# Moving one tile's q and k loads from SyncE's DMA queue into GpSimd's, in a fused retention and Mish MLP kernel on one Trainium2 core

## The chip, the cores and the metric

The kernel runs on one core of a Trainium2 chip. A core has TensorE (matrix products and transposes), VectorE, ScalarE (casts and activations), GpSimd (elementwise work on SBUF) and SyncE (here only an issuer of DMAs). DMAs are issued by an instruction in the queue of SyncE, ScalarE or GpSimd; 16 DMA engines move the data of all of them. In this kernel a DMA that casts float32 to bfloat16 on the way is always issued by GpSimd.

The metric is the device time of one execution in microseconds (us). Each engine runs its own instructions in the order in which they are issued; waits between engines are semaphores. In the profile PE is TensorE, PEld its weight loads, DVE is VectorE, ACT is ScalarE, POOL is GpSimd, SP is SyncE. `q0` in the DMA view is the queue that GpSimd feeds, `q1` the one that SyncE feeds.

## What is computed

```python
# q, k, v: (8 batches, 8 heads, 576 positions, 64), float32
scores = (1 / sqrt(64)) * q @ k.T
gamma  = 1 - 2.0 ** (-5 - arange(8))                 # one per head
Dmat   = where(i >= j, gamma ** (i - j), 0)
attn   = (scores * Dmat) @ v                         # retention, no softmax
x      = attn.transpose(0, 2, 1, 3).reshape(4608, 512)
h      = x @ w_in                                    # w_in (512, 2048)
out    = (h * tanh(softplus(h))) @ w_out             # Mish; w_out (2048, 512), out float32
```

## The kernel before

The 576 positions of a batch are cut into chunks of 128 (the last one has 64, and two batches share one). 36 chunks in all make nine tiles of four chunks, that is 512 rows of `x` each. Tiles 0 and 1 are the first chunks of the eight batches. They need no state from earlier positions, only scores times the decay mask times v. All others are computed with a running state: `state` (L359) multiplies k and v of a chunk (L373), and `step_o` adds q times the state.

For every tile follow two products. `g1(t, f)` (L407) computes 128 of the 2048 hidden columns in four matmuls of 512 rows (L412) and lets ScalarE apply Mish (L414); 16 calls make a tile. `g2` multiplies by `w_out`, for tile 0 in `g2_first` (L438, matmuls L444): here `part` 0 to 3 needs one quarter of `w_out` each, for all four chunks of the tile.

**Tile 0.** SyncE and ScalarE load q and k of tile 0 in pieces of one head (L124 to L127), GpSimd loads five of k's heads with a cast (`load_first_k`, L103, the tile `kb`), then SyncE loads v (L128, `load_first_v(0)`). Casts, transposes (`f_transpose`), scores and masks (`f_scores`) follow. `f_v(0, b, engine)` (L260) casts v of batch b to bfloat16, for b 0 to 2 on GpSimd and for b 3 on ScalarE; `f_out(0, b)` (L265) multiplies and copies the result to `xT`, the left side of `g1`.

**Weights.** GpSimd loads `w_in` with a cast in five DMAs: columns 0 to 255, 256 to 511, and three times 512 (L497 to L504, issued by L86). The casts of v stand between the first ones in GpSimd's queue. `w_out` follows in four DMAs of four row blocks each (L508, issued by L89).

**Tile 1.** `load_second_qk` (L107) issues 16 DMAs of 128 KB on SyncE, in two groups g of four heads: four of q and four of k for each group, all float32. They land in `stage`, a tile with the name `gT`, which held tile 0's q and k and then its masked scores; so they wait for `f_out(0, ...)`. `s_cast(g)` (L226) casts a group on VectorE, `s_transpose(g)` (L234, matmuls L239) transposes it, `s_scores` (L246) multiplies and masks. Tile 1's v comes in four DMAs of 256 KB by GpSimd (`load_first_v(1)`, L511), and `f_v(1, b)` casts it on ScalarE.

**Order on TensorE.** After tile 0's 16 `g1` calls comes the loop at L523, with tile 0's 16 `g2_first` calls and between them the steps for tile 1: `T0` (transposes of group 0) ahead of call 0, `S0 C1` (scores of group 0, cast of group 1) ahead of call 3, `T1` ahead of 9, `S1` ahead of 11, v's casts ahead of 12, the four `f_out(1, ...)` ahead of 14 and 15. Then follow tile 1's `g1` calls, with the first chunks of the later tiles between them.

**GpSimd's queue.** After the `w_in` and `w_out` issues it holds `make_masks` (four small operations), `load_first_v(1)`, `load_k0(0)` (k of batch 0 with positions in the partitions, for the first state), and for b 0 to 3 `f_state(0, b)` (L281, v scaled for the state, L285) and `load(8 + b)` (three DMAs: q, k, v of one later chunk, L303). `step_v` (L316) and more loads follow, one chunk at a time.

Of the kernel before, what the change touches and what calls it, by code (L numbers as in the profile page):

```python
# [10 lines left out]
F32 = mybir.dt.float32  # L11
# [6 lines left out]
def kernel(  # L18
# [18 lines left out]
    nc = tc.nc  # L37
    B, H, S, D = q.shape
    assert (B, H, S, D) == (8, 8, 576, 64)
    P = 128  # L40
# [3 lines left out]
    nF = d_ff // P  # L44
# [40 lines left out]
    def load_w_in(f0, n):  # L85
        nc.gpsimd.dma_start(out=w_in_t[:, :, ds(f0, n)], in_=w_in_r[:, :, ds(f0, n)])  # L86

    def load_w_out(i):
        nc.gpsimd.dma_start(out=w_out_t[:, ts(i, 4), :], in_=w_out_r[:, ts(i, 4), :])  # L89
# [4 lines left out]
    stage = gp.tile([P, nF, NCH * P], BF16, name="gT")  # L94
    raw = {0: (stage[:, 0:H, :].bitcast(F32), stage[:, H:nF, :].bitcast(F32))}
# [8 lines left out]
        for h in hs:  # L104
            nc.gpsimd.dma_start(out=kb0[:, h, :], in_=rows(k, 0, h))

    def load_second_qk():  # L107
        raw[1] = (stage[:, H:nF, :].bitcast(F32), stage[:, 0:H, :].bitcast(F32))
        for g in range(2):
            for i, x in enumerate((q, k)):  # L110
                for p in (2 * g, 2 * g + 1):
                    for e in range(2):
                        to = raw[1][i][:, ds(2 * p, 2), :].rearrange("(j e) a c -> j e (a c)", e=2)
                        nc.sync.dma_start(
                            out=to[:, e],
                            in_=x[4:8, 2 * p + e, 0:P, :].rearrange("b (g r) d -> g b (r d)", r=8))

    def load_first_v(t):
        for b in range(4 * t, 4 * t + 4):
            v0[b] = io.tile([P, H, D], F32, name="vraw", bufs=8)  # L120
            (nc.gpsimd if t else nc.sync).dma_start(out=v0[b], in_=v[b, :, 0:P, :].rearrange("h p d -> p h d"))
# [46 lines left out]
    def make_masks():  # L168
        nc.gpsimd.memset(mask, 1.0)
        nc.gpsimd.affine_select(out=mask, in_=mask, compare_op=OP.is_ge, fill=0.0,  # L170
                                base=0, pattern=[[1, P]], channel_multiplier=-1)
        nc.gpsimd.tensor_copy(mask2, mask)
        nc.gpsimd.memset(mask2[0:64, 64:P], 0.0)

    def keep_warm(n, pool=ps_o, name="ops"):
        idle = pool.tile([P, 512], F32, name=name)
        for _ in range(n):
            nc.tensor.matmul(idle, lhsT=zeros[:, 0:P], rhs=zeros, start=True, stop=True)
# [81 lines left out]
    def f_v(t, b, copy):  # L260
        vb = first.tile([P, H, D], BF16, name="vb", bufs=4)
        copy(vb, v0[4 * t + b])
        fst[t]["vb"][b] = vb

    def f_out(t, b, copy):  # L265
        if b == 0:
            xts[t] = xp.tile([P, KC, NCH * P], BF16, name="xT")
        vb = fst[t]["vb"][b]
        if t == 0 and b < 2:
            pool, name = ((ps_st, "st"), (ps_o, "ops"))[b % 2]  # L270
            ot = pool.tile([P, NP, P], F32, name=name)
        else:
            ot = ps_sc.tile([P, 2, NP, P], F32, name="sc")[:, 0]
        for p in range(NP):
            for e in range(2):
                nc.tensor.matmul(ot[ds(64 * e, 64), p, :], lhsT=vb[:, 2 * p + e, :],
                                 rhs=fst[t]["sm", 2 * p + e][:, b, :],
                                 start=(p == 0), stop=True, skip_group_check=True)
        copy(xts[t][:, :, ts(b, P)], ot)

    def f_state(t, b, engine=nc.gpsimd):  # L281

        n = 4 * t + b
        v0s[n] = first.tile([P, H, D], BF16, name="v0s", bufs=B)
        engine.tensor_tensor(v0s[n], v0[n], gv[:, 0, :].unsqueeze(2).to_broadcast([P, H, D]), op=OP.mult)  # L285

    def load_k0(b):
        k0[b] = first.tile([P, H, D], BF16, name="k0", bufs=B)
        nc.gpsimd.dma_start(out=k0[b], in_=k[b, :, 0:P, :].rearrange("h p d -> p h d"))  # L289
# [3 lines left out]
    def load(n):  # L293
        if n >= n_chunks:
            return
        b, c = chunks[n]
        qr = io.tile([P, H, D], F32, name="qraw")
        vr = io.tile([P, H, D], F32, name="vraw", bufs=8)
        qks = io.tile([P, 2, H, D], BF16, name="qks", bufs=9)
        live[n] = {"q": qr, "v": vr, "qks": qks}  # L300
        for t, src in ((qr, q), (qks[:, 1], k), (vr, v)):
            if c < 4:
                nc.gpsimd.dma_start(  # L303
                    out=t, in_=src[b, :, ds(P * c, P), :].rearrange("h p d -> p h d"))
            else:
                for e in range(2):
                    nc.gpsimd.dma_start(  # L307
                        out=t[ds(64 * e, 64)],
                        in_=src[b + e, :, ds(512, 64), :].rearrange("h p d -> p h d"))
# [167 lines left out]
    dve, act, pool = nc.vector.tensor_copy, nc.scalar.copy, nc.gpsimd.tensor_copy  # L477
# [16 lines left out]
            f_cast(n, act)  # L494
    keep_warm(3, ps_h, "hp")
    nc.scalar.activation(warm, pos[:, 0:1], AX.Mish)
    load_w_in(0, 256)  # L497
    f_v(0, 0, pool)
    f_v(0, 1, pool)
    load_w_in(256, 256)  # L500
    f_v(0, 2, pool)
# [2 lines left out]
        load_w_in(512 * i, 512)  # L504
    for b in range(4):
        f_out(0, b, (dve, act)[b % 2])
    load_second_qk()
    for i in range(4):  # L508
        load_w_out(i)
    make_masks()  # L510
    load_first_v(1)  # L511
    load_k0(0)
    for b in range(4):
        f_state(0, b)
        load(N0 + b)
    nc.vector.tensor_scalar(gq, gq, 1.0 / math.sqrt(D), None, op0=OP.mult)


# [32 lines left out]
    for u in range(24):  # L551
        j, w = divmod(u, 4)
# [99 lines left out]
```

## Time and profile before

| | us |
|---|---|
| median of three runs | 317.65 |
| lowest and highest of them | 316.12, 317.86 |
| the profiled execution | 316.29 |
| its span, first to last instruction | 314.6 |
| TensorE busy | 300.1 |
| VectorE, ScalarE, GpSimd busy | 133.6, 113.5, 139.2 |

The share of the 16 DMA engines that was busy, and the work of TensorE, by stage of the span:

| stage (us from the span's start) | what TensorE does | TensorE busy, us | DMA share | GB/s |
|---|---|---|---|---|
| 0 to 18.26 | tile 0's retention | 11.77 | 1.02 | 195 |
| 18.26 to 34.39 | tile 0's `g1` | 14.26 | 1.17 | 258 |
| 34.39 to 53.44 | tile 0's `g2_first`, tile 1's retention | 18.20 | 1.31 | 213 |
| 53.44 to 165 | later tiles, loads still running | 110.66 | 1.38 | 179 |
| 165 to 314.6 | later tiles | 145.19 | 0.51 | 83 |

The granted TensorE clock is 1.00 in every stage. The DMA share adds the time of all packets and divides it by 16 engines, so packets that overlap on one engine can bring it above 1. A landing is the moment at which a DMA's semaphore tells that its data is there; the DMA view gives the time from issue to landing.

### The profile page before, as it was taken

To read this page: it belongs to the slowest core of one execution; us is meant where nothing else is said; L and a number is where in the kernel's file an instruction comes from. 1 tells how busy PE (TensorE), PEld (TensorE's weight loads), DVE (VectorE), ACT (ScalarE), POOL (GpSimd) and SP (SyncE) were. 2 spreads that over 40 slices of the span, in tenths; PEclk is the share of its full clock that TensorE was granted. 3 is DMA by queue.
4 is the path that set the end of the run, shared out by engine and by line. 5 is a ranking of instruction groups with operands and counts; after the bars stand their busy time and mean duration, and the time that the engine had idled before them with its cause. 6 is when DMAs were issued, how large, how long until landed. Compare 5 with 4: busy or idle time off the path is not lost.

```text
span 314.6 us, 5797 instructions
## 1 busy us (share of the span) xinstructions
PE 300.1 (95%) x2404; PEld 151.5 (48%) x2443; DVE 133.6 (42%) x191; ACT 113.5 (36%) x190; POOL 139.2 (44%) x172
## 2 busy tenths in 40 slices
PE   5877999999999999999999999999999999999995
PEld 2533544555554554444444454545454544444444
DVE  2711257389735535453535453535354332001011
ACT  5755416753254533333333323232333233333300
POOL 5682459998993986456554445332010000000000
PEclk9999999999999999999999999999999999999999
DMA  7999999999996999999999979990614000010031
GB/s 176 234 192 280 231 225 219 273 180 146 220 221 121 145 189 188 159 134 203 136 166 133 180 130 162 136 150 33 98 38 102 34 35 33 35 33 33 35 100 67
DMA packets 79354, 44.10 MB, mean 140 GB/s; under 512 B 63072, under 2 KB 69984, under 8 KB 79328
## 3 DMA queue, kind: packets, MB, share of 16 engines
q0 software_dynamic: 47904, 24.98, 63.2%
q1 hardware_dynamic: 30848, 18.23, 28.6%
q10 hardware_dynamic: 576, 0.52, 0.6%
q8 instruction: 19, 0.31, 0.5%
q14 instruction: 7, 0.06, 0.1%
HBM read 38.80 MB, written 9.44 MB: 153 GB/s over the span
## 4 chain that ended last, share of the span: by engine, by line
PE 88%; DMA 8%; POOL 1%; issue 1%; DVE 1%; SPq 0%; ACT 0%; ACTq 0%
PE hp L412 36%; PE ops L427 30%; DMA w_in_t<-in_moe_w_in_dram 5%; PE hp L427 4%; PE sc L341 3%; PE st L373 2%; PE hp L444 2%; PE sc L393 2%; PE sc L398 2%; DMA vraw<-in_v_dram 2%; DMA gT<-in_k_dram 1%; PE sc L328 1%; PE st L444 1%; PE hp L455 1%; PE ops L444 1%
## 5 line engine op out<-in xcount | busy, mean ns | idle before, releaser
L412 PE MATMUL hp<-xT,w_in_t 128*128 128x512 bf16 x546 | 141.0, 380 | 3.8 <-DMA w_in_t<-in_moe_w_in_dram 1.8
L414 ACT ACTIVATE gT<-hp 128x512 bf16<-128x512 f32 x144 | 86.1, 598 | 157.1 <-PE hp L412 145.1
L427 PE MATMUL ops<-w_out_t,gT 128*128 128x512 bf16 x430 | 110.1, 379 | 0.4
L412 PEld LDWEIGHTS <-w_in_t 128*128 128x128 bf16 x576 | 53.6, 98 | 64.7 <-DMA w_in_t<-in_moe_w_in_dram 3.0
L427 PEld LDWEIGHTS <-gT 128*128 128x128 bf16 x496 | 48.3, 98 | 58.0 <-issue 0.8
L463 DVE COPY res<-ops 128x512 f32<-128x512 f32 x28 | 19.3, 688 | 83.4 <-PE ops L427 79.6
L376 DVE TENSOR_TENSOR ssb<-st,diag 128x512 bf16<-128x512 f32 x32 | 21.9, 685 | 46.6 <-PE st L373 46.6
L319 POOL TENSOR_TENSOR vs<-vraw,gv 128x512 bf16<-128x512 f32 x28 | 30.2, 1089 | 20.2 <-issue 13.9
L303 POOL DMA_DIRECT2D qraw<-in_q_dram x24 | 22.3, 930 | 36.3 <-DVE qks L313 34.7
L345 DVE TENSOR_TENSOR sm<-sc,mask 128x1024 bf16<-128x1024 f32 x28 | 33.0, 1216 | 6.4 <-PE sc L341 6.4
L303 POOL DMA_DIRECT2D vraw<-in_v_dram x24 | 21.9, 914 | 2.3 <-DMA w_out_t<-in_moe_w_out_dram 1.9
L303 POOL DMA_DIRECT2D qks<-in_k_dram x24 | 21.9, 911 | 1.8 <-DMA w_out_t<-in_moe_w_out_dram 1.8
L313 DVE TENSOR_TENSOR qks<-qraw,gq 128x512 bf16<-128x512 f32 x28 | 18.7, 705 | 0.0
L402 DVE CAST xT<-sc 128x512 bf16<-128x512 f32 x24 | 15.3, 681 | 0.0
L427 PE MATMUL hp<-w_out_t,gT 128*128 128x512 bf16 x61 | 14.7, 379 | 0.2
L329 ACT COPY qkT<-sc 128x1024 bf16<-128x1024 bf16 x10 | 10.1, 1010 | 8.0 <-PE sc L328 8.0
L307 POOL DMA_DIRECT2D qraw<-in_q_dram x8 | 5.6, 708 | 13.9 <-DVE qks L313 13.9
L393 PE MATMUL sc<-qkT,ssb 128*64 128x128 bf16 (+1 forms) x224 | 9.5, 213 | 0.0
L398 PE MATMUL sc<-sm,vs 128*64 128x128 bf16 x192 | 9.4, 219 | 0.0
L341 PE MATMUL sc<-qkT 64*128 64x128 bf16 x224 | 9.0, 218 | 0.0
L444 PEld LDWEIGHTS <-gT 128*128 128x128 bf16 x64 | 5.8, 98 | 6.5
L289 POOL DMA_DIRECT2D k<-in_k_dram x8 | 7.4, 926 | 3.5 <-DMA w_out_t<-in_moe_w_out_dram 3.5
(99 smaller groups left out, 192.4 us busy)
## 6 DMA issues: line engine op xcount, KB each, us to landing
out_dram<-res SPq DMA_DIRECT2D x31, 256.0 KB, 3.9
vraw<-in_v_dram POOLq DMA_DIRECT2D x28, 256.0 KB, 7.3
qraw<-in_q_dram POOLq DMA_DIRECT2D x24, 256.0 KB, 5.4
qks<-in_k_dram POOLq DMA_DIRECT2D x24, 128.0 KB, 6.3
w_out_t<-in_moe_w_out_dram POOLq DMA_DIRECT2D x4, 512.0 KB, 21.2
gT<-in_q_dram SPq DMA_DIRECT2D x15, 128.0 KB, 6.0
w_in_t<-in_moe_w_in_dram POOLq DMA_DIRECT2D x3, 512.0 KB, 10.5
gT<-in_k_dram SPq DMA_DIRECT2D x9, 128.0 KB, 6.0
```

The costliest lines, as they stand in the source:

```text
L303: nc.gpsimd.dma_start(out=t, in_=src[b, :, ds(P * c, P), :].rearrange("h p d -> p h d"))
L313: nc.vector.tensor_tensor(live[n]["qks"][:, 0], live[n]["q"], gq[:, c, :].unsqueeze(2).to_broadcast([P, H, D]), op=OP.mult)
L319: nc.gpsimd.tensor_tensor(vs, live[n]["v"], gv[:, c, :].unsqueeze(2).to_broadcast([P, H, D]), op=OP.mult)
L341: nc.tensor.matmul(sc[:, e, p, :], lhsT=qk[r, 1, p, :], rhs=qk[r, 0, p, :], start=True, stop=True)
L345: nc.vector.tensor_tensor(sm.rearrange("p e n i -> p (e n) i"), sc.rearrange("p e n i -> p (e n) i"), m.unsqueeze(1).to_broadcast([P, 2 * ...
L376: nc.vector.tensor_tensor(ssb.rearrange("p e n d -> p e (n d)"), st.rearrange("p n d -> p (n d)").unsqueeze(1).to_broadcast([P, 2, NP * 64 ...
L393: nc.tensor.matmul(ot[ds(64 * e, 64), p, ds(i0, iw)], lhsT=st_sb[bb, cc][:, e, p, :], rhs=qk[:, 0, p, ds(i0, iw)], start=(i0 == 0 and p == ...
L412: nc.tensor.matmul(hp, lhsT=w_in_t[:, c, ts(f, P)], rhs=xts[t][:, c, :], start=(c == 0), stop=(c == KC - 1))
L414: nc.scalar.activation(gts[t][:, f, :], hp, AX.Mish)
L427: nc.tensor.matmul(ops, lhsT=gts[t][:, f, ts(s, P)], rhs=w_out_t[:, f, :], start=(f == 0), stop=(f == nF - 1))
L444: nc.tensor.matmul(outs[0, s], lhsT=gts[0][:, f, ts(s, P)], rhs=w_out_t[:, f, :], start=(f == 0), stop=(f == nF - 1))
L463: copy(ot, ops)
```

## The change

All of it concerns the first part of the kernel.

1. `f_v(0, 0, pool)` stands ahead of `load_w_in(0, 256)` in GpSimd's queue.
2. `load_second_qk` issues on GpSimd's queue instead of SyncE's, and takes the group as its argument.
3. The order of GpSimd's queue behind the `w_in` issues is new: masks; the four `f_state(0, b)`; eight DMAs of tile 1's q and k, group 0; `w_out` 0 and 1; eight DMAs of group 1; `w_out` 2 and 3; tile 1's v; then the loads of the four later chunks, with `load_k0(0)` behind the first of them.

No arithmetic is changed, and no transfer is added or left out.

```diff
-    def load_second_qk():
-        raw[1] = (stage[:, H:nF, :].bitcast(F32), stage[:, 0:H, :].bitcast(F32))
-        for g in range(2):
-            for i, x in enumerate((q, k)):
-                for p in (2 * g, 2 * g + 1):
-                    for e in range(2):
-                        to = raw[1][i][:, ds(2 * p, 2), :].rearrange("(j e) a c -> j e (a c)", e=2)
-                        nc.sync.dma_start(
-                            out=to[:, e],
-                            in_=x[4:8, 2 * p + e, 0:P, :].rearrange("b (g r) d -> g b (r d)", r=8))
+    raw[1] = (stage[:, H:nF, :].bitcast(F32), stage[:, 0:H, :].bitcast(F32))
+
+    def load_second_qk(g):
+        for i, x in enumerate((q, k)):
+            for p in (2 * g, 2 * g + 1):
+                for e in range(2):
+                    to = raw[1][i][:, ds(2 * p, 2), :].rearrange("(j e) a c -> j e (a c)", e=2)
+                    nc.gpsimd.dma_start(
+                        out=to[:, e],
+                        in_=x[4:8, 2 * p + e, 0:P, :].rearrange("b (g r) d -> g b (r d)", r=8))
...
+    f_v(0, 0, pool)
     load_w_in(0, 256)
-    f_v(0, 0, pool)
     f_v(0, 1, pool)
     load_w_in(256, 256)
     f_v(0, 2, pool)
...
         load_w_in(512 * i, 512)
     for b in range(4):
         f_out(0, b, (dve, act)[b % 2])
-    load_second_qk()
-    for i in range(4):
-        load_w_out(i)
     make_masks()
-    load_first_v(1)
-    load_k0(0)
     for b in range(4):
         f_state(0, b)
+
+    for g in range(2):
+        load_second_qk(g)
+        load_w_out(2 * g)
+        load_w_out(2 * g + 1)
+    load_first_v(1)
+    for b in range(4):
         load(N0 + b)
+        if b == 0:
+            load_k0(0)
```

## The prediction

> **What bounds the kernel now.** I read the page's slices first, then the chain of waits, TensorE's timeline from 13 to 54 us, GpSimd's timeline beside it, and the DMA view in narrow windows.
>
> ```profile
> PE   5877999999999999999999999999999999999995
> DMA  7999999999996999999999979990614000010031
> ```
>
> A slice is 7.9 us. TensorE is full from the fifth slice on; in the first four it is not, while the DMA engines are. By stage TensorE is busy 11.77 of the first 18.26 us, 14.26 of 16.13 us up to 34.39, 18.20 of 19.05 us up to 53.44, and then 255.9 of 261.2 us. Only what happens before about 54 us can pay, and the chain says what sets that part:
>
> ```profile
> 15.95 14.78 DMA w_in_t<-in_moe_w_in_dram
> 30.77 3.63 PE hp L412 x16
> 34.39 0.89 PE sc L239 x16
> ```
>
> The last `w_in` block lands at 30.72 and releases the last four row blocks of `g1`. TensorE's timeline (start, length, idle time before and its releaser in brackets):
>
> ```profile
> 17.17 0.41 PE L276 MATMUL sc<-gT,vb 128*64 128x128 bf16 x8 [1.19 <-ACT vb L262]
> 18.26 7.07 PE L412 MATMUL hp<-xT,w_in_t 128*128 128x512 bf16 x31 [0.68 <-ACT xT L279]
> 25.78 3.63 PE L412 MATMUL hp<-xT,w_in_t 128*128 128x512 bf16 x16 [0.45 <-DMA w_in_t<-in_moe_w_in_dram]
> 30.77 3.63 PE L412 MATMUL hp<-xT,w_in_t 128*128 128x512 bf16 x16 [1.36 <-DMA w_in_t<-in_moe_w_in_dram]
> 34.23 0.61 PE L239 MATMUL sc<-ident,qb 128*128 128x128 bf16 x8
> 35.14 1.90 PE L444 MATMUL hp<-w_out_t,gT 128*128 128x512 bf16 x7
> 42.72 0.81 PE L444 MATMUL hp<-w_out_t,gT 128*128 128x512 bf16 x3
> ```
>
> Four blocks f of `g1` take 3.63 us. Waits for `w_in`: 0.45 + 1.36 = 1.81 us. Before `g1` stands the cast of tile 0's fourth v (ScalarE idle 2.01 us for it, until 16.50). L444 at 42.72 is the first use of the third `w_out` block, 7.58 us after the first use of the first.
>
> ```profile
> q0 software_dynamic: 1302, 1.29, 63.4%
> q1 hardware_dynamic: 1247, 2.05, 52.7%
> ```
>
> This is the DMA view from 22 to 34 us (packets, MB, share): GpSimd's queue (q0) has little over half of the engines, SyncE's second q and k the rest. So the fourth and fifth `w_in` DMA (two of 256 columns, then three of 512) land 4.1 and 5.0 us after the one before (21.6, 25.7, 30.7), while `w_out` blocks of the same size, with nothing beside them, land every 2.65 us (35.1 to 43.0, mean).
>
> ```profile
> 16.68 3.00 POOL L89 DMA_DIRECT2D w_out_t<-in_moe_w_out_dram  x4
> 26.02 1.37 POOL L121 DMA_DIRECT2D vraw<-in_v_dram  x1 [3.25 <-DMA w_in_t<-in_moe_w_in_dram]
> 31.01 0.88 POOL L121 DMA_DIRECT2D vraw<-in_v_dram  x1 [3.62 <-DMA w_in_t<-in_moe_w_in_dram]
> 35.38 0.88 POOL L289 DMA_DIRECT2D k<-in_k_dram  x1 [3.49 <-DMA w_out_t<-in_moe_w_out_dram]
> 37.92 0.93 POOL L303 DMA_DIRECT2D qraw<-in_q_dram  x1 [0.59 <-DMA w_out_t<-in_moe_w_out_dram]
> ```
>
> GpSimd's timeline has the fact that I take to decide. Counting its DMAs (5 kb, 5 w_in, 4 w_out, 4 v, k0, q): the 17th, issued at 26.02, waits for the 9th, which landed at 25.7 (its issue plus its time to landing, as for all landings here); the 18th for the 10th (30.7, 0.3 earlier); the 19th for the 11th (35.1); the 20th for the 12th (37.6). **Eight of this queue's DMAs are in flight at most**, and the ninth holds the queue until the first has landed.
>
> **The change, step by step.**
>
> *Cast of v ahead of the first w_in half.* v's first block landed at 6.74 + 4.6 = 11.3, so the cast starts near 11.4 and the half's DMA 0.56 later (as 12.63 to 13.19), at 12.0 instead of 10.77: +1.2. The second half moves 0.1, its cast waiting for v (12.58) as now. Only 0.08 MB of GpSimd's queue moved before 14 us, under v's 0.33 MB, which is some 0.4 us at the 0.36 MB per 2 us that follow. The `w_in` stream shifts by 0.1 to 1.2; I take 0.4. In exchange the fourth v need not share its last 1.6 us: it lands between 15.0 (11.3, 12.6, and two more spacings) and 16.5; at 15.2, and with the 1.76 us from the cast's start to `g1` as now, `g1` could start at 17.0. The half itself landed at 10.77 + 6.1 = 16.9, now 17.3. `g1` starts at 17.35 instead of 18.26.
>
> *No second q and k beside w_in.* The third `w_in` DMA lands at 21.6 + 0.4 = 22.0, the fourth and fifth each 2.65 later: 24.65 and 27.3 (at 3.4, the third's spacing now, 28.8). The wait moves forward: f 0 to 3 end at 20.98, TensorE idles 1.05 to 22.05, and the other twelve f (10.9) run through: `g1` ends at 32.95 instead of 34.39, **-1.45**. The four state scalings (4 x 1.05) and masks (1.2) follow the `w_in` issues on GpSimd, from 17 to 22.4; hidden, since the queue needs its next DMA only when `w_in` has moved, near 26. Without that cover they would cost 4.2.
>
> *Second q and k in GpSimd's queue.* 16 DMAs; the nearest issue costs are kb's 0.55 and L303's 0.93; I take 0.55, kb's being the plainer form. They are the 11th to 18th and 21st to 28th, two `w_out` blocks between. The 11th to 17th issue from 22.4 to 26.3, in time. The 18th, the last k of the first half, waits for the fifth `w_in`: 27.3 + 0.3 = 27.6. A DMA of 128 KB that meets an idle queue lands after 2.8 (at 201 us), so 30.4; its cast (0.69 to 1.06) is done by 31.5, before the transposes at 32.95. At 0.6 per DMA (v's 1.2 per 256 KB) instead of 0.34 (SyncE's 0.75 at 52.7% of 117%) the eight land by 32.1 and cost 0.3.
>
> *w_out.* Its first block is issued at 27.6 + 0.55 = 28.15. What 512 KB need after the queue ran dry no row shows: 2.8 - 0.6 + 2.65 = 4.9 from 128 KB, 4.0 - 1.2 + 2.65 = 5.5 from q's 256 KB (at 185 us), 6.4 from `w_in`'s second half (5.0 for 256 KB, + 1.4) in a busy queue. I take 5.2, between the two nearest: 33.35. The transposes end at 33.85, so no wait here: first L444 at 33.85 instead of 35.14, and the third block is wanted at 33.85 + 7.58 = 41.43. The second block lands at 36.0. But the 28th DMA waits for just that block: 36.3; the third `w_out` block is queued behind it, 36.85, with only that 128 KB left in the queue ahead, and lands at 36.85 + 5.2 = **42.05** (41.75 to 43.25). TensorE waits 0.65 there: 42.1 instead of 42.72.
>
> The DMA page of the Trainium skill ("DMA: Bandwidth & Descriptors", section "Anatomy of one DMA — SWDGE (gpsimd) path") gives for a DMA issued from GpSimd 2.0 us plus bytes over 436 GB/s. By it, my estimate is 3.2 us for that block, which then lands at 40.1 and the wait is gone: -1.3 instead of -0.6. The measured 2.8 for 128 KB, where the page would have 2.3, speaks against it. The same page (section "SWDGE vs HWDGE vs iDMA") sends plain transfers to SP or ACT, against this change; no run here shows the same transfer from both queues.
>
> *The rest, at nothing.* SyncE loses 16 issues (17.62 to 29.5); it has nothing else before its store at 50.48. The fourth `w_out` block lands at 44.7, wanted at 47.0; v at 45.9 to 49.5, its last cast wanted at 51.3; the first chunk's q at 50.7 (now 50.0), wanted at 52.5; the second's at 55.6, for VectorE, which after the first two scalings (53.15, 1.38) idles until 58.68; k0 near 54.5 (behind the first chunk now), wanted by L373 at 58.56. Later chunks load some 2 us later: the third to fifth chunk's q land at 56.1, 60.4, 65.2 and are scaled at 61.01, 66.80, 71.95, so 4.9 us of slack or more hide it. If that cover were gone, the 2 us would show in full.
>
> **Sum**: 42.1 - 42.72 = -0.6, bounds: -1.5 (stream shift 0.1, dry-queue block 4.9) to +0.8 (`w_in` spacing 3.4, so that all behind it comes 1.5 later; 6.4 for one of the two blocks gives +0.5). The profiled execution is 316.29 (span 314.6); the three others are 316.12, 317.65, 317.86. The median of the three is 317.65, 1.36 above the profiled one. I set the forecast against the mean of all four, 316.98: **316.4** us, own range 315.4 to 317.8.
>
> **Rivals.** *The dry queue doesn't bite* (chance 0.23). v lands early, `g1` starts at 17.0, the third `w_in` lands by 21.3, so that TensorE reaches the third `w_out` block at 21.35 + 10.9 + 0.9 + 7.58 = 40.7, and the block is there: 40.7 - 42.72 = -2.0: 315.0. For it: the 1.81 us of `w_in` waits and 1.19 for the cast are real. Against it: eight in flight, seen four times.
>
> *The eight-in-flight limit costs more than the sharing did* (0.22, slower). Place: the 18th and 28th DMA, which let the queue run dry twice. If each `w_out` block after it takes 6.4 instead of 5.2, the first lands at 34.55 and the third at 34.55 + 2.65 + 0.85 + 6.4 = 44.45: +1.75; with `w_in` at 3.4, or issues at 0.93 (the seven before the 28th), up to +3. Middle +2: 319.0. It decides once the third block lands after 44.3 (+1.6). For it: small DMAs go out one per landing here, where SyncE's queue had eight of its own beside GpSimd's eight. Against it: the limit stands in the way of only two blocks.
>
> *Given back later* (0.05): `g1` is 1.4 us sooner, but v or the first chunks are just as much later: 317.0.
>
> **How the numbers follow.** Forecast 0.50. About 0.5% (1.6 us) is what a measurement of this kernel can tell from no change. The forecast gives faster 0.07, same 0.40, slower 0.03; the first rival 0.20 and 0.03 same; the second 0.20 slower and 0.02 same; the last 0.05 same. Faster 0.27, same 0.50, slower 0.23. Range 314.8 to 319.0, to the middle of both rivals.
>
> **What would show it.** q1 is gone between 18 and 50 us; the waits of L412 fall from two of 1.81 to one near 22 us of about 1; GpSimd's timeline shows the 18th and 28th DMA held until 0.3 us after the fifth `w_in` and the second `w_out` landed; L444 has a new wait near 41.5, released by `w_out`. Wrong if L239 waits for casts, if L444's first matmul comes later than 35.1, if the third `w_out` block lands before 41 or after 44.3, or if TensorE idles beyond 54 us.

## The result, and the profile after

The changed kernel takes **320.28 us** (median of 4 runs, 319.90 to 320.68), the kernel before 317.20 (4 runs on the same chip, 316.12 to 317.86): a ratio of **1.0101, with a 95% interval of 1.0065 to 1.0136**. The change costs about 3.1 us, more than the 0.5% that can be told from no change. The profiled execution of after took 319.90 us (span 318.2), 3.6 more than that of before by both.

The page's slices of after, TensorE's busy tenths, its granted clock and the DMA share (a slice is 8.0 us):

```profile
PE   5779967999999999999999999999999999999995
PEclk9779999999999999999999999999999999999999
DMA  7998999999999699999999999991333200010031
```

The fourth and fifth slice are now as full as the later ones: the waits for `w_in` are gone. In their place there are a 6 and a 7 in the sixth and seventh slice (40 to 56 us). TensorE's timeline of after tells where (start, length, idle time before and its releaser in brackets):

```profile
18.24 15.66 PE L412 MATMUL hp<-xT,w_in_t 128*128 128x512 bf16 x63 [0.68 <-ACT xT L279]
33.74 0.61 PE L239 MATMUL sc<-ident,qb 128*128 128x128 bf16 x8
34.63 1.89 PE L444 MATMUL hp<-w_out_t,gT 128*128 128x512 bf16 x7
...
44.85 0.81 PE L444 MATMUL hp<-w_out_t,gT 128*128 128x512 bf16 x3 [2.50 <-DMA w_out_t<-in_moe_w_out_dram]
...
55.70 0.41 PE L276 MATMUL sc<-sm,vb 128*64 128x128 bf16 x8 [1.31 <-ACT xT L279]
...
56.92 1.24 PE L412 MATMUL hp<-xT,w_in_t 128*128 128x512 bf16 x5
```

`g1` of tile 0 runs through, from 18.24 to 33.9, and L444 begins at 34.63 instead of 35.14: 0.5 us gained. Then the third `w_out` block is missing for 2.50 us, so that its first matmul stands at 44.85 instead of 42.72: the gain has become a loss of 2.1. A second new wait, 1.31 us at the last step of tile 1's `f_out`, makes it 3.6: tile 1's `g1` begins at 56.92. In the same view of before it begins here (the 53.44 given above is from the chain of waits, which counts from the end of the matmul ahead of it and has 57.09 in after):

```profile
53.29 2.76 PE L412 MATMUL hp<-xT,w_in_t 128*128 128x512 bf16 x11
```

From there to the end of the span both kernels need 261.3 us, so the rest of the kernel neither gives nor takes.

GpSimd's timeline of after shows what made the third block late, in the same columns:

```profile
28.26 0.50 POOL L114 DMA_DIRECT2D gT<-in_k_dram  x1 [2.27 <-DMA w_in_t<-in_moe_w_in_dram]
28.75 1.75 POOL L89 DMA_DIRECT2D w_out_t<-in_moe_w_out_dram  x2
30.50 2.17 POOL L114 DMA_DIRECT2D gT<-in_q_dram  x4
...
38.35 0.50 POOL L114 DMA_DIRECT2D gT<-in_k_dram  x1 [2.80 <-DMA w_out_t<-in_moe_w_out_dram]
39.34 1.88 POOL L89 DMA_DIRECT2D w_out_t<-in_moe_w_out_dram  x2 [0.49 <-DMA gT<-in_q_dram]
41.21 3.65 POOL L121 DMA_DIRECT2D vraw<-in_v_dram  x4
```

The 18th DMA goes out at 28.26, 0.28 us after the landing of the 10th (the fifth `w_in` block, 27.98); the 28th at 38.35, 0.28 after that of the 20th (the second `w_out` block, 38.07); the 29th, the third `w_out` block, waits once more, for the 21st, and is issued at 39.34. It lands at 44.81. Eight DMAs in flight are the limit of this queue here as in the kernel before. The traces also show where the eight comes from: GpSimd's DMAs announce their landings on eight semaphores (110 to 117) in turn, and a DMA is held until the one that last used its semaphore has landed; SyncE's DMAs use eight others in the same way. So the number may belong to the way this program is built and not to the queue; no run here changed it.

The DMA view from 26 to 46 us, in 40 slices of half a microsecond, with the row of GpSimd's queue (packets, MB, share); first that of before:

```profile
DMA  9999999999999999999999999999999999999999
q0 software_dynamic: 3264, 3.47, 98.2%
```

And the same view of after:

```profile
DMA  9999722744999999699999999989225999999569
q0 software_dynamic: 2538, 3.77, 91.6%
```

Before, the DMA engines had work in every slice, and SyncE's queue moved 1.41 MB beside GpSimd's 3.47. After, GpSimd's queue is alone, and it runs dry twice, that is, it has next to nothing left to move: from 28 to 31 us, before the first `w_out` block, and from 40 to 41.5, before the third. Such a place has 1 us nearly without work, but what is behind it lands later by more, since 5.47 us pass from the third block's issue to its landing.

The chain of waits of after has the same story in six steps (start, length, what):

```profile
16.18 11.80 DMA w_in_t<-in_moe_w_in_dram
28.76 1.74 POOL w_out_t L89 x2
30.50 8.56 DMA gT<-in_q_dram
39.34 1.88 POOL w_out_t L89 x2
41.22 2.76 POOL vraw L121 x3
43.97 10.07 DMA vraw<-in_v_dram
```

It no longer ends at a `w_in` block at 30.72 and TensorE from there. It alternates between a landing and GpSimd's issue that waited for it, up to v's last block at 54.04.

### The profile page after: what moved, and what is told of

Read it like the earlier page. It is cut to its first block, busy times and chain, and to the rows that moved or that the text cites. A ratio compares the mean times of both kernels' runs of the same rounds, so it can differ in the third digit from the quotient of the medians.

```text
span 318.2 us, 5800 instructions
## 1 busy us (share of the span) xinstructions
PE 300.7 (95%) x2404; PEld 151.5 (48%) x2443; DVE 132.3 (42%) x191; ACT 113.7 (36%) x190; POOL 147.1 (46%) x188
## 3 DMA queue, kind: packets, MB, share of 16 engines
q1 hardware_dynamic: 29568, 16.13, 27.3%
## 4 chain that ended last, share of the span: by engine, by line
PE 81%; DMA 13%; POOL 4%; issue 1%; ACT 1%; ACTq 0%; SPq 0%; DVE 0%
PE hp L412 35%; PE ops L427 30%; DMA vraw<-in_v_dram 5%; PE hp L427 4%; DMA w_in_t<-in_moe_w_in_dram 4%; DMA gT<-in_q_dram 3%; PE sc L341 3%; PE st L373 2%; PE sc L393 2%; PE sc L398 2%; DMA gT<-in_k_dram 2%; PE sc L328 1%; POOL w_out_t L89 1%; PE hp L455 1%; POOL w_in_t L86 1%; POOL vraw L121 1%
## 5 line engine op out<-in xcount | busy, mean ns | idle before, releaser
L412 PEld LDWEIGHTS <-w_in_t 128*128 128x128 bf16 x576 | 54.3, 99 | 63.5 <-issue 3.0
L376 DVE TENSOR_TENSOR ssb<-st,diag 128x512 bf16<-128x512 f32 x32 | 21.9, 686 | 47.3 <-PE st L373 47.3
L427 PE MATMUL hp<-w_out_t,gT 128*128 128x512 bf16 x61 | 14.7, 379 | 0.2
L444 PEld LDWEIGHTS <-gT 128*128 128x128 bf16 x64 | 5.8, 97 | 9.2 <-issue 2.8
L444 PE MATMUL hp<-w_out_t,gT 128*128 128x512 bf16 x29 | 7.4, 379 | 2.6 <-DMA w_out_t<-in_moe_w_out_dram 2.5
```

The lines of the kernel that those rows point to most:

```text
L376: nc.vector.tensor_tensor(ssb.rearrange("p e n d -> p e (n d)"), st.rearrange("p n d -> p (n d)").unsqueeze(1).to_broadcast([P, 2, NP * 64 ...
L412: nc.tensor.matmul(hp, lhsT=w_in_t[:, c, ts(f, P)], rhs=xts[t][:, c, :], start=(c == 0), stop=(c == KC - 1))
L427: nc.tensor.matmul(ops, lhsT=gts[t][:, f, ts(s, P)], rhs=w_out_t[:, f, :], start=(f == 0), stop=(f == nF - 1))
```

## The experiments

Three accounts were to be told apart first. **A**: the eight DMAs in flight, with many small ones ahead of large ones, let the queue run dry. **B**: the granted clock, since after's profile has two stretches at half clock. **C**: the bytes that GpSimd's queue now carries. Later ones (D, E) have their letters in the expectations of the runs that test them.

### The second q and k back on SyncE, all else as changed

```diff
-                    nc.gpsimd.dma_start(
+                    nc.sync.dma_start(
```

> The changed kernel with tile 1's sixteen q and k DMAs back in SyncE's queue; the cast of v ahead of the first w_in half and the new order of the rest of GpSimd's queue stay. Theory A, eight of GpSimd's DMAs in flight at most: without the sixteen, the w_out blocks are the 11th to 14th DMA and are issued by 26 us, the third lands by 44, v's last block by 49, TensorE has no wait at the third w_out block; w_in shares the engines again and its last block lands near 31. Time 316.5 to 318.0. Rival B, the clock: the half clock from 19.0 to 22.4 us that the later w_in half brings about is what costs the time; it stays with v first, and the time stays at 319.5 or above. Rival C, plain loads are dearer through GpSimd's queue whatever their number: 316.5 to 318.0, as A.

Measured: 318.21 us (12 runs), before 318.17 (29 runs on that chip), ratio 1.0001 (0.9982 to 1.0021). That is 0.2 above the range of A and C, on a chip where the kernel before takes 1 us more than above; as a ratio, the loss is gone, and with it the wait for `w_out`. Waits for `w_in` are back, three of them (1.76, 1.15 and 1.41 us). B had the time stay at 319.5 or more, and falls. The profiled clock is 0.989, as in after, but with the half clock elsewhere, from 7.4 to 14.3 us. The base of before further down shows B's stretch without the loss: it runs at half clock from 8.6 to 12.1 and from 18.9 to 22.3, as after does at nearly the same times. The parts that stay (v first, state scaling and masks ahead) cost nothing that can be measured.

### Only k back on SyncE

```diff
-                    nc.gpsimd.dma_start(
+                    (nc.sync if i else nc.gpsimd).dma_start(
```

> The changed kernel with k's eight DMAs of tile 1 in SyncE's queue and q's eight in GpSimd's. Theory A: the w_out blocks become the 15th, 16th, 21st and 22nd DMA of GpSimd's queue and wait for the 7th, 8th, 13th and 14th, so the queue does not run dry; the third w_out block lands by 43.5, and the time is 315.5 to 317.8. Rival C: half of the dear loads are left, and half of the loss stays, 318.2 to 319.0. Rival B, the clock: 319.5 or above.

Measured: 317.13 us (12 runs), ratio 0.9962 (0.9940 to 0.9984): quicker than both kernels. TensorE's timeline:

```profile
22.33 3.63 PE L412 MATMUL hp<-xT,w_in_t 128*128 128x512 bf16 x16 [1.42 <-DMA w_in_t<-in_moe_w_in_dram]
27.05 7.25 PE L412 MATMUL hp<-xT,w_in_t 128*128 128x512 bf16 x32 [1.09 <-DMA w_in_t<-in_moe_w_in_dram]
...
42.60 0.81 PE L444 MATMUL hp<-w_out_t,gT 128*128 128x512 bf16 x3
...
53.18 1.04 PE L412 MATMUL hp<-xT,w_in_t 128*128 128x512 bf16 x4
```

Eight q DMAs are still in GpSimd's queue, yet the third `w_out` block is there when TensorE comes for it (42.60, no bracket), and tile 1's `g1` begins at 53.18. Half of the moved bytes without any of the loss: C falls as a price by the byte. The `w_out` blocks are the 15th, 16th, 21st and 22nd DMA here, and the queue does not run dry. Why this kernel is 0.4% quicker than before is not shown by its profile: tile 1's `g1` begins only 0.1 us earlier, and the span is 315.0 us against 314.6.

### The order of v and w_in alone, in the kernel before

```diff
-    load_w_in(0, 256)
     f_v(0, 0, pool)
+    load_w_in(0, 256)
```

> The kernel before with one part of the change alone, the cast of v's first block ahead of the first w_in half. Theory A: the half lands 0.5 later, g1 starts within 0.3 us of where it did, the rest is as before: within 0.7 us of the kernel before, 316.4 to 317.9. Rival B, the clock: the later start brings a stretch of half clock that costs 1.5 to 3 us, 318.7 to 320.2.

Measured: 318.42 us, between the ranges of A and B; against before on that chip (318.17) the ratio is 1.0010 (0.9988 to 1.0033): the same. In its profiled run `g1` starts at 17.81 instead of 18.26, and the waits for `w_in` behind it are 1.21, 0.71 and 1.34 us instead of 0.45 and 1.36. An earlier `g1` reaches a block that is no earlier.

### The same bytes in twice as many DMAs

```diff
-                    nc.gpsimd.dma_start(
-                        out=to[:, e],
-                        in_=x[4:8, 2 * p + e, 0:P, :].rearrange("b (g r) d -> g b (r d)", r=8))
+                    for s in range(2):
+                        nc.gpsimd.dma_start(
+                            out=to[ds(32 * s, 32), e],
+                            in_=x[4:8, 2 * p + e, ds(64 * s, 64), :].rearrange("b (g r) d -> g b (r d)", r=8))
```

> The changed kernel with each of the sixteen q and k DMAs of 128 KB cut in two of 64 KB, the same bytes in the same order: 32 DMAs. Theory A: sixteen stand between the fifth w_in and the first w_out block, nine of them behind the fifth w_in's landing (28.0), then one issue of 0.5 us after another: the first w_out block is issued near 33 and lands near 38.5 instead of 34.5; ten of the second group wait for the first and second w_out block, so the third is issued near 47 and lands near 52 instead of 44.8. Time 326 to 329. Rival C, cost by bytes and queue and not by the number of DMAs: 319.5 to 321.

Measured: 330.90 us (2 runs), ratio 1.0404 (1.0352 to 1.0456), beyond the upper end of A's figure. The largest waits by line, 15 to 62 us (us in total, times, longest; L445 is L444 of after):

```profile
PE hp L445 <- DMA w_out_t<-in_moe_w_out_dram: 10.0, 2, 6.9
...
POOL gT L115 <- DMA w_out_t<-in_moe_w_out_dram: 5.3, 2, 3.5
```

TensorE waits 10 us for `w_out`, and GpSimd's small DMAs wait for the landing of `w_out` blocks ahead of them. The third block is issued at 48.90 and lands at 56.05. With the bytes as they were and the number doubled, the loss against before went from 1.0% to 4.0%: the number of DMAs counts, and C falls once more. But the number has two prices here, which this run does not part. One is the place among the eight in flight. The other is the issue: behind the fifth `w_in` block nine small DMAs go out one after another, 0.5 us each (28.23 to 33.30), and only then the first `w_out` block. The size was put too low: the `w_out` blocks landed 6.54 and 7.15 us after their issue, where 5.5 and 5 were reckoned.

### A base without DMA transposes

The seven kernels from here on make all transposes of q and k on TensorE, where before and after leave those of the later chunks to DMAs. That adds some 7 us behind the stretch of interest. The edit below is the one that counts; the branch with the DMA transpose is also gone.

```diff
-    NPE = 18
+    NPE = 36
```

Here is the kernel before on this base:

> The kernel before with the transposes of the later 18 chunks, which SyncE's DMA transposes did, on TensorE as for the first ones (eight transposes and a copy for each chunk). A base for what follows; nothing before 100 us differs. Eight transposes take TensorE 0.45 us net in the trace of before, so 18 x 0.45 = 8 us more: 325 to 327.5.

And the changed kernel:

> The changed kernel with the same edit (all transposes on TensorE). Theory A (eight of GpSimd's DMAs in flight, a cost before 57 us alone): the loss stays what it was, 2.0 to 4.0 us above c1. Rival E (part of the loss sits behind 57 us, where loads, stores and DMA transposes share the engines): less than 2.0 above c1.

Measured: 325.14 us (ratio to the kernel before 1.0220, 1.0193 to 1.0248) and 328.89 us (1.0338, 1.0305 to 1.0370). The change costs 3.75 us on this base too, so the later transposes are no part of it, and E falls.

### Which dry place costs

Group 0 or group 1 of the second q and k on SyncE, the other one in GpSimd's queue; the second edit in turn:

```diff
-                    nc.gpsimd.dma_start(
+                    (nc.gpsimd if g else nc.sync).dma_start(
```

> The changed kernel with group 0's eight q and k DMAs on SyncE and group 1's on GpSimd, all transposes on TensorE: the first dry place is gone, the second is left. Theory A (eight in flight): the first two w_out blocks are the 11th and 12th DMA, queued early, and land 2.65 apart; the 20th, the last k of group 1, waits for the second w_out block, the queue runs dry, the third w_out block lands 5.2 to 6.5 after that and the fourth 3.5 to 4.5 later; w_in shares the engines with 1 MB and ends near 30. TensorE reaches the third block at 43 and waits up to 1 us; v's last block lands near 51. 325 to 327 (c1 325.1, c2 328.9). Rival D (a w_out block that follows another takes 3.6 to 4.4 us whatever stood in the queue): the first two blocks land 3.6 or more apart.

```diff
-                    nc.gpsimd.dma_start(
+                    (nc.sync if g else nc.gpsimd).dma_start(
```

> The changed kernel with group 0's eight DMAs on GpSimd and group 1's on SyncE, all transposes on TensorE: the first dry place is left, the second is gone. Theory A: the 18th DMA waits for the fifth w_in, which shares with SyncE's 1 MB and lands near 30; the first w_out block is issued near 31 and lands near 36.5, the second 3.5 later; TensorE waits 1.5 to 2 us at the first w_out block and not at the third, which is the 21st DMA and waits for the 13th. 326 to 328. If the second dry place alone costs, whatever the sharing, the time is under 325.5.

Measured: 325.57 us (1.0238, 1.0207 to 1.0269) with group 0 on SyncE, 0.4 above the base of before; 327.42 us (1.0316, 1.0267 to 1.0366) with group 1 there, 2.3 above. The intervals tell the second from the base of before, but not the first. Both times are in the ranges of A. TensorE's timeline of the kernel with group 0 on SyncE (L441 is L444):

```profile
43.83 1.02 PE L441 MATMUL hp<-w_out_t,gT 128*128 128x512 bf16 x4
```

And of the one with group 1 there:

```profile
37.89 1.90 PE L441 MATMUL hp<-w_out_t,gT 128*128 128x512 bf16 x8 [1.98 <-DMA w_out_t<-in_moe_w_out_dram]
```

With the dry place at the third block, that block lands at 43.78, just when it is wanted, because TensorE comes late: it waited 1.95 us for `w_in` and ran at half clock from 23.4 to 26.8. With the dry place at the first block, that block lands at 37.84 and TensorE stands 1.98 us for it. In the first kernel the first two `w_out` blocks, with no dry place ahead of them, land 2.98 us apart (33.73, 36.71), nearer to the 2.65 of the kernel before than to the 3.56 of after, so D, which had 3.6 or more there, falls. A dry place costs what TensorE has to wait there: nothing at the third block of the first kernel, 1.98 us at the first block of the second, and in after nothing at the first block and 2.50 us at the third.

### Without tile 1's v

```diff
+            if t:
+                v0[b] = v0[b - 4]
+                continue
```

> The changed kernel, all transposes on TensorE, without the four loads of tile 1's v: tile 1 takes tile 0's v, so that part of the result is another one; 1 MB less is moved, and no instruction on TensorE, VectorE or ScalarE is left out. Theory A: of the 3.5 us lost by 57 us, 2.1 are the wait at the third w_out block, and 1.4 are v, 4.5 us later than forecast behind the fourth block; without v's loads the wait at f_out(1, ...) goes and the first is left: 1.2 to 1.6 us less than c2, 327.3 to 327.7. If v's lateness is covered by the wait for w_out, the time stays at c2's 328.9; if the 1 MB is what costs, it falls to c1's 325.

Measured: 328.51 us (1.0331, 1.0299 to 1.0364), against 328.89 (1.0338) with v: no gain that can be told. Theory A's figure was missed; the run's second case, v covered by the wait for `w_out`, is the one that fits. TensorE's timeline of the changed kernel's base (L441 and L239 are L444 and L239 of after):

```profile
45.28 1.24 PE L441 MATMUL hp<-w_out_t,gT 128*128 128x512 bf16 x3 [3.26 <-DMA w_out_t<-in_moe_w_out_dram]
46.74 1.06 PE L239 MATMUL sc<-ident,qb 128*128 128x128 bf16 x8 [0.22 <-issue]
```

And of this kernel (L444 and L242 are those two lines):

```profile
46.00 1.86 PE L444 MATMUL hp<-w_out_t,gT 128*128 128x512 bf16 x4 [3.10 <-DMA w_out_t<-in_moe_w_out_dram]
47.66 1.06 PE L242 MATMUL sc<-ident,qb 128*128 128x128 bf16 x8
```

In both, the eight transposes behind the long wait take 1.06 us instead of 0.61. The windows view of the changed kernel's base says why (window, length, busy times of PE, PEld, DVE, ACT and POOL with their instructions, granted clock, DMA share, GB/s):

```profile
45.50:48.90 3.40, 3.18 (x21) 2.30 (x21) 0.21 (x1) 0.00 (x0) 2.25 (x3) 0.50 1.14 225
```

It is the same in that of the kernel without v:

```profile
45.20:48.60 3.40, 2.60 (x13) 1.48 (x13) 0.00 (x0) 0.00 (x0) 2.76 (x4) 0.50 1.10 165
```

A wait of over 3 us is followed by 3.4 us at half clock. From the first use of the third `w_out` block to tile 1's `g1` the kernel before needs 53.29 - 42.72 = 10.6 us, the changed one 12.1 (full clock, 1.31 us of wait for v), its base without DMA transposes 12.0 (half clock, no wait for v), and the kernel without v 11.8 (half clock). The further 1.3 to 1.5 us thus come either from v or from the clock; each covers the other. That v costs them alone is not shown.

### Better orders

In the first, q stays in GpSimd's queue and k on SyncE, held back there by a one-column memset behind the state scaling:

```diff
+        nc.gpsimd.memset(raw[1][1][:, 4 * g, 0:1], 0.0)
...
-                    nc.gpsimd.dma_start(
+                    (nc.sync if i else nc.gpsimd).dma_start(
```

> Test of a better order, all transposes on TensorE: q of tile 1 on GpSimd, k on SyncE as in the run with k on SyncE (e2), and k's DMAs held back by a memset of one column of their target in GpSimd's queue, behind the four state scalings (near 22 us) for group 0 and behind the second w_out block for group 1. Theory A: no dry queue, and less sharing: the fourth w_in lands by 25.5 and the fifth by 29.5, TensorE's waits for w_in fall from e2's 2.5 to about 1.4 us. Against c1: 1.6 to 2.8 us less, where e2 had 1.0 to 1.2 less than the kernel before. If sharing with w_in is not what is left, 1.0 to 1.2 less than c1.

The second has in addition the first `w_in` half ahead of v again, as in the kernel before:

```diff
-    f_v(0, 0, pool)
     load_w_in(0, 256)
+    f_v(0, 0, pool)
```

> The same as e7, with the first w_in half ahead of the cast of v as in the kernel before. Theory A: the third w_in lands 0.7 earlier (21.6) and g1 starts up to 0.7 later, so the wait at it goes: 0 to 0.7 us below e7. If having v early is worth more, it is above e7.

Measured: 323.95 us (1.0184, 1.0156 to 1.0213) and 323.15 us (1.0161, 1.0132 to 1.0191), 1.2 and 2.0 below the base of before (325.14). The first fell short of Theory A's 1.6 to 2.8; its 1.2 is the figure given for the case that sharing with `w_in` is not what is left. The second has the lowest median on this base, but the two intervals overlap. Its profile has `g1` in one piece, at half clock from 18.5 to 21.9 us, which hides a wait of some 0.8 us for the third `w_in` block (an estimate: it landed at 22.94, and f 0 to 3 at full clock would have ended at 18.52 + 3.63 = 22.15), and only 0.46 us of wait for the first `w_out` block:

```profile
18.52 15.65 PE L410 MATMUL hp<-xT,w_in_t 128*128 128x512 bf16 x63 [0.68 <-ACT xT L280]
...
35.53 1.90 PE L442 MATMUL hp<-w_out_t,gT 128*128 128x512 bf16 x7 [0.46 <-DMA w_out_t<-in_moe_w_out_dram]
...
43.25 0.81 PE L442 MATMUL hp<-w_out_t,gT 128*128 128x512 bf16 x3
```

So the aim of the change can be had. With the DMA transposes kept, the fastest kernel that ran is the one with k alone back on SyncE, 0.4% below the kernel before; the two held-back orders were not tried with them.

## Why the prediction was wrong

**The mechanism was right.** The limit of eight in flight, the two places where it bites (18th and 28th DMA), the issue 0.3 us after the landing waited for, the end of the two `w_in` waits and the new wait of L444 for `w_out` are all in the profile of after. The forecast failed in three sizes; its second rival, slower by this same mechanism "once the third block lands after 44.3", had 0.22, and it was the case that came: 44.81. It came by another sum, though: the rival put 6.4 us for a `w_out` block behind each dry place, and 5.76 and 5.47 were measured.

**"What 512 KB need after the queue ran dry ... I take 5.2 ... The second block lands at 36.0"** is the step that failed most. The third block was to land at 42.05 and did at 44.81, 2.76 late, which is a sum of five terms: the fifth `w_in` block 27.98 instead of 27.3 (+0.7); the first `w_out` block another 0.5 later (34.51 instead of 33.35); **the second 3.56 us after it instead of 2.65** (+0.9); the 29th DMA waiting for the 21st too, where 0.55 of issue was reckoned (+0.4); the third block 5.47 us after its issue instead of 5.2 (+0.3). The dry-queue price itself was nearly right. The spacing was not: 2.65 was the mean of a queue in which large blocks followed one another without a break. It was 3.56 and 4.39 in after, 4.00 and 3.23 with 32 DMAs, 3.38 and 3.79 in the kernels with one group on SyncE. The DMA view between two such landings, the row of GpSimd's queue (packets, MB, share), tells what moved meanwhile. Before, 35.09 to 37.64 us:

```profile
q0 software_dynamic: 522, 0.52, 122.3%
```

After, 34.51 to 38.07 us:

```profile
q0 software_dynamic: 608, 0.89, 114.9%
```

A block is 0.52 MB. In before as much moves in the time between; in after the engines are nearly as busy and move 0.37 MB more, of the small DMAs in flight behind the block. The second held-back order has the same spacing without any dry place: its first two `w_out` blocks land 4.00 us apart (35.48 to 39.48), with the DMA engines busy throughout and 1.02 MB moved:

```profile
q0 software_dynamic: 731, 1.02, 116.2%
```

So a dry place is not needed for a long spacing, and the bytes of the DMAs behind the block are a part of it. They are not all: with k alone on SyncE 2.78 us had 0.79 MB, and with group 1 on SyncE 3.38 us had 0.63 MB. What sets the spacing is open.

The range for the third block was made from 41.75 to 43.25 by taking one bound at a time. But the terms lie in one chain, each landing releasing the next issue, so that errors of one sign add: three of 0.3 to 0.5 and two of 0.7 to 0.9 made 2.8. Because TensorE's due time was fixed by then, all of it past the due time showed: a wait of 2.50 us instead of 0.65.

**"The rest, at nothing"** failed as well. v was put at 45.9 to 49.5, its last cast wanted at 51.3; it landed at 50.42 to 54.04, 4.5 later, since it stands behind the `w_out` blocks in the same queue. ScalarE's timeline:

```profile
54.06 0.62 ACT L262 CAST vb<-vraw 128x512 bf16<-128x512 f32 x1 [0.53 <-DMA vraw<-in_v_dram]
```

The wait of 1.31 us before 55.70 follows from this cast. A cover of 1.8 us for v was taken as enough, while the prediction's own slower rival had the third `w_out` block, ahead of v in the queue, 2.4 us later (44.45 instead of 42.05). As told above, where that wait is missing, the half clock behind the longer one costs as much, so the price of the 1.3 to 1.5 us is shown and its owner is not. The chunks' q later on cost nothing, as foretold: the first is there at 55.35.

**"g1 starts at 17.35", "-1.45"**: v's fourth block was no earlier (cast at 16.48, before 16.50), so `g1` started where it had. The two waits for `w_in` behind it are gone, as foretold; the one of 1.05 us near 22 that was to remain did not show, because in this execution the first f's ran at half clock. ScalarE's timeline of after has the Mish activations 1.6 to 1.7 us apart there (the first is at 19.40), where before has 0.9:

```profile
21.10 0.60 ACT L414 ACTIVATE gT<-hp 128x512 bf16<-128x512 f32 x1 [1.11 <-PE hp L412]
22.71 0.60 ACT L414 ACTIVATE gT<-hp 128x512 bf16<-128x512 f32 x1 [1.01 <-PE hp L412]
```

The windows view of after has the clock (0.50, the third figure from the right):

```profile
19.00:22.40 3.40, 3.40 (x10) 1.22 (x8) 0.00 (x0) 1.20 (x2) 3.40 (x5) 0.50 1.20 192
```

Hence 0.5 gained and not 1.45. An estimate parts the missing 0.95. At full clock f 0 to 3 would have ended by 21.9 and waited for the third `w_in` block, which landed at 22.59; the twelve f behind it take 10.53 us at full clock (a row of the first held-back order), so `g1` would have ended near 33.2 instead of 33.9. Then 0.7 are the clock, the rest the later block, and the start of `g1` cost nothing. None of this moved the end: the third `w_out` block's landing depends on GpSimd's queue, and TensorE waited 2.50 us for it anyway.

The profiled run of before had no such stretch (mean clock 0.998), other runs of it have: over 29 of them the mean clock was 0.976 to 1.000, over four of after 0.989 to 0.995, and one stretch of 3.4 us at half clock takes 0.005 off the mean (1.7 of 318 us). So the 3.6 us between the two profiles are one pair of executions; the medians are 3.1 apart.

**The two rules of the Trainium skill.** The fit of "DMA: Bandwidth & Descriptors" (section "Anatomy of one DMA — SWDGE (gpsimd) path") would have had the third block 3.2 us after its issue; 5.47 were measured with the queue dry, so the row was the better guide. The same page's advice to send plain transfers to SP or ACT (section "SWDGE vs HWDGE vs iDMA") is borne out in part: with q and k from GpSimd 1.0101, from SyncE 1.0001, but with k alone from SyncE 0.9962, the lowest of the three.

## What to carry to other kernels

A queue that keeps eight DMAs in flight is loaded by their number, not only by their bytes: a run of small DMAs ahead of large ones can let it run dry, and the next large block then comes late. So count the DMAs ahead of each block that is waited for, and the landings that their issues wait for. Here it was best to leave eight of the small transfers in the queue of the large blocks and to put the other eight on SyncE's; all sixteen on either queue were slower. Holding k's back by a data dependence gave no more that can be told (1.2 us below its base, where the same split without it was 1.0 below the kernel before). When a forecast is a chain of landings that release issues, add the bounds along the chain instead of taking the largest.

## What the runs showed of the hardware that was not expected

Two 512 KB blocks next to each other in GpSimd's queue landed 2.4 to 4.4 us apart: 2.55 us with 0.52 MB moved between the landings (before), 3.56 with 0.89 (after), 4.00 with 1.02 in a queue that never ran dry (second held-back order), but also 2.78 with 0.79 (k alone on SyncE) and 3.38 with 0.63 (group 1 on SyncE). Such a spacing has to be taken as a range; no run here tells what sets it.

A wait of TensorE of 3.1 to 3.3 us was followed by 3.4 us at half clock in two kernels, and in the kernel with 32 DMAs waits of 3.18 and 6.87 us went with half clock too (39.8 to 43.2, 53.4 to 60.2). The 2.50 us in after were not followed by it (clock 1.00 from 44.85 to 48.30), while 1.95 us in the kernel with group 0 on SyncE were (23.4 to 26.8), and the stretch at 19.0 in after came with waits of 1.37 and 0.68 us before it. The stretches of one execution begin whole multiples of 3.41 us apart: 8.79 and 19.03 in after, 7.98, 18.22 and 45.52 in its base without DMA transposes (3 and 11 times). The Trainium skill ("TensorE: Matmul & The Clock Gate", part "The HAM clock gate (the "warmup" mystery)") has the clock set by activity in free-running windows of 3.41 us, which agrees with this grid and with waits of like length being dear in one execution and not in another; how much idle time a window needs is not settled by these runs. For these kernels it means that a wait of 3.1 to 3.3 us can cost 4.4 to 4.7, if the half clock behind it is not covered (3.10 + 1.26 without v, 3.26 + 1.46 in the changed kernel's base, both against the 10.57 us that the kernel before needs from there to tile 1's `g1`).
